# Two decode layers on one Trainium2 core: two more units of a V kept in place, w2 in six places, and the loads of the next K and wq cut in other pieces

## The chip, the cores and the metric

The kernel runs on one core of one Trainium2 chip. The metric is the device time in microseconds (us) of that core. Every program has one launch, and the times are medians of a few runs.

## The reference, cut to what matters

One token (B = 1, one query position, D = 512) goes through two layers of the same weights. Each layer is an attention block and a dense block, each with a layer norm in front and a residual sum behind. All numbers are float32.

```python
def A(x, k_cache, v_cache, wq, wo):          # 32 heads, 4096 keys, 128 wide
    q = (x @ wq).reshape(B, Sq, H, Dh).transpose(0, 2, 1, 3)
    p = softmax(einsum("bhqd,bhkd->bhqk", q, k_cache) * Dh ** -0.5)
    o = einsum("bhqk,bhkd->bhqd", p, v_cache)
    return o.transpose(0, 2, 1, 3).reshape(B, Sq, H * Dh) @ wo

def B(x, w1, b1, w2, b2):                    # 1376 hidden
    return gelu_tanh(x @ w1 + b1) @ w2 + b2

for layer in range(2):
    x = x + A(layernorm(x))
    x = x + B(layernorm(x))
```

The K and V caches have 64 MB each and are read by both layers, so nearly all of the work is reading them.

## The kernel before, in words

**Tiling.** The heads are taken in 8 groups (g = 0 to 7) of 4. The K of a group is one block of 128 partitions by 16384 floats (BLOCK, 8 MB), and so is its V. A block is 8 chunks of NC = 2048 floats (1 MB), a chunk is 4 units of U = 512 floats (256 KB). For each group the kernel makes the queries, multiplies them with the chunks of K (`scores`, L232, on TensorE), takes the softmax (L236 to L254, with the exponential on ScalarE in L244), weighs V with it, sums over the keys and multiplies with the group's wo into the PSUM bank pB (`head_out`). Layer 0 takes the groups upward; layer 1 takes them downward, 7, 6, 5 and so on, so that what layer 0 had last is still in SBUF. Groups in the middle weigh V on ScalarE and VectorE (L269, L274) and sum it there (L279); the first two of layer 1 and the last two of each layer multiply it on TensorE (`values`, L262).

**The arena.** All large data lies in one SBUF tensor, `arena`, addressed by hand: three blocks, of which the third ends early and goes over into the places SPARE (2 chunks), HELD (w1) and PAIR (2 chunks, a wo and a wq). At the end of layer 0 the K of group 7 lies in chunks 0 to 7, its V in chunks 8 to 15, and the V of group 6 (the second last) from chunk 16. Its first five chunks (STAY) stay there until layer 1 needs them. Of the rest, KEPT = 6 units are carried over: five are copied by ScalarE into the PSUM banks pK (L540) and one into pB (L606), since w2, w1 and others take their places in the meantime. In layer 1 they are copied back to the places in V1_HOME: pB's by L506 during the first group's softmax, pK's by L484. What was not kept is loaded again (L482).

**The change of layer.** At the end of layer 0 SP loads, in this order, the last pieces of V, wo, and then w1 in three parts and w2 in five (W2_PARTS), of 11 blocks of one unit. w2 lies in SPARE, in eight places (W2_AT, block c in place c % 8); the third of five parts waits for the reading of `row` (the sum of the heads, L332), which lies in place 7. `mlp` multiplies the 11 blocks (L414), with some idle products in between that keep TensorE busy. `follow` names loads that are issued behind the product of a block: with block 3, 5, 7 and 9 go the last two parts of w2 and into the places that came free the first chunk of the K of group 6 and the wq of group 6. Then layer 1 begins: `set_x` (L166, L167), four query blocks of 8 products each (L199) with wq of group 7, which lies in PAIR's second chunk, and between the second and the third the product of the mean (`minus_mean`, L178), the centred x and its squares (L185, L186). `first_queries` transposes the products (L205) and takes the mean off (L206); `rstd_of` has the product of the variance (L175). Then come the scores of group 7, 64 products in all.

**Order.** All loads are issued by SP into one queue, with `load` holding them in the written order. A load waits until what lay at its target has been read. Instructions marked `pin` stay behind whatever was written before them on their engine; all others are ordered by the framework, ahead of time, by when they are ready and by how late they may be. Each engine then runs its list in order, so what stands behind a waiting instruction waits too. The products of L199 and the four of the mean are not pinned, L175 and the scores are. DMAs take turns on eight semaphores, so a load also waits for the eighth before it.

Of the kernel before, what the change touches and what calls it, by code (L numbers as in the profile page):

```python
# [21 lines left out]
G = 8  # L22
# [6 lines left out]
KEPT = 6  # L29

# [11 lines left out]
K2_HOME = 12 * NC  # L42

V1_HOME = *(2 * BLOCK + NC * c for c in range(5)), 8 * NC, 6 * NC, 7 * NC
W2_AT = tuple(SPARE + U * (c % 8) for c in range(FB)), tuple(U * c for c in range(FB))
# [15 lines left out]
def decode_layers(ctx: ExitStack, tc: tile.TileContext, k, v, w, w1, w2, out):  # L61
# [33 lines left out]

    def of_w(first, n):

        row, i = first
        return w[row][:, AHEAD + NC * i : AHEAD + NC * (i + n)]
# [7 lines left out]
    def free_now(layer, n):  # L107

        if layer == 0:
            at = HELD + 2 * NC  # L110
        elif n == 0:
            at = 6 * NC
            return arena[:, at : at + U], arena[:, 11 * NC : 11 * NC + 4 * 129]
        else:
            at = 9 * NC if n == 1 else 14 * NC
# [65 lines left out]
    def mean_of(xs, s, at, whole=False, xc=None):  # L181
        nm = minus_mean(s, at, whole)
        sq, ss = small("sq", 4), small("ss")
# [3 lines left out]
        return nm, ss, xc  # L187
# [23 lines left out]
    def queries(n, xc, wt, at, t=None, short=False, between=None):  # L211
        t = wt[:, 0, :] if t is None else t
        pin(nc.vector.tensor_scalar(t, wt[:, 0, :], xc[:, 0:1], None, op0=ALU.mult))
        for c in range(1, 4):
            pin(nc.vector.scalar_tensor_tensor(t, wt[:, c, :], xc[:, c : c + 1], t, op0=ALU.mult, op1=ALU.add))  # L215
# [14 lines left out]
    def scores(z, c, kt):  # L230
        for j in range(J):
            pin(nc.tensor.matmul(pS[32 * j : 32 * j + C, :], z[:, j, C - 1 - c : 2 * C - 1 - c],  # L232
                                 kt[:, j, :], start=(c == 0), stop=(c == C - 1)))
# [206 lines left out]
    for layer in range(2):  # L440
# [4 lines left out]
        else:  # L445
            for c in range(4):
                query_block(c, xs, wq_first)
                if c == 1:
                    nm, ss, xc = mean_of(xs, s, pN[:, 0:1])
        if layer == 1:  # L450
            for a in (0, NC // 2):
                load(PAIR + NC + a, part(k, order[1], 1, 2)[:, a : a + NC // 2])
            here["k", order[1], 1] = chunk(arena[:, PAIR + NC : PAIR + 2 * NC])
            negm = small("negm")
            nc.vector.tensor_copy(negm, nm)
            z = first_queries(negm)
# [7 lines left out]
        for n, g in enumerate(order):  # L464
# [13 lines left out]
            elif layer == 1 and n == 1:  # L478
                tiles = [(c, here["k", g, c]) for c in range(2)]
                tiles += list(stream("k", g, ((2, 3), (3, 4), (4, 8)), -2 * NC))  # L480
                n_kept = STAY + U * KEPT
                load(V1_HOME[6] + n_kept % NC, v[g][:, n_kept:BLOCK])  # L482
                for u in range(STAY, n_kept - U, U):
# [30 lines left out]
            elif layer == 1 and n == 1:  # L514
# [3 lines left out]
                for pieces, base in ((((0, 4),), K2_HOME), (((4, 6),), SPARE - 4 * NC)):  # L518
# [169 lines left out]
```

## Time and profile before

| what | us |
|---|---|
| median of 3 runs | 675.73 |
| the runs | 673.7 to 676.0 |
| span of the profiled execution | 671.6 |
| TensorE busy | 299.7 |
| VectorE busy | 407.1 |
| ScalarE busy | 215.4 |

The profiled execution's own time is recorded as its span, 671.6 us from the first to the last instruction; nothing around it is in the trace. The core read 284.92 MB, 424 GB/s over the span. Times below are in us from the start of the span. The change of layer lies between about 342 and 415. Rows give, where they are of DMAs, the moment of issue; the landing is that moment plus the time to landing.

### The profile page before, as it was taken

How to read it: one execution, taken by the hardware profiler on the slowest of the kernel's cores; microseconds unless marked ns; L12 is line 12 of the kernel's file. 1: busy time of each engine (PE TensorE's matmuls, PEld its weight loads, DVE VectorE, ACT ScalarE, POOL GpSimd, SP SyncE). 2: the span in 40 equal slices, each digit the busy share in tenths (PEclk: the TensorE clock that was granted, in tenths of full speed). 3: DMA queues.
4: the chain of work that ended last, by engine and by line, in shares of the span. 5: the costliest groups of instructions: out<-in, count | busy, mean ns of one | idle time of the engine just before them, and what ended most of it. 6: DMA issues, size and time to landing. Idle time of an engine off the chain costs nothing.

```text
span 671.6 us, 6013 instructions
## 1 busy us (share of the span) xinstructions
PE 299.7 (45%) x2236; PEld 79.7 (12%) x2236; DVE 407.1 (61%) x510; ACT 215.4 (32%) x697; POOL 5.2 (1%) x26
## 2 busy tenths in 40 slices
PE   1511703415116053165768986704316025065597
PEld 1000100101001010011114311101001001011124
DVE  3059679498696886971322313288597694973513
ACT  0047074190560823802011200083290650910010
POOL 1000000000000000000000000000000000000000
PEclk9965755757558557578689998655757559557799
DMA  9999999999999999999999999999999999999997
GB/s 377 437 437 438 435 437 437 403 461 437 437 437 397 444 426 434 433 429 426 425 415 399 422 422 438 437 433 433 431 433 437 437 430 402 462 426 414 431 414 286
DMA packets 11556, 285.29 MB, mean 425 GB/s; under 512 B 1284, under 2 KB 1288, under 8 KB 3720
## 3 DMA queue, kind: packets, MB, share of 16 engines
q1 hardware_dynamic: 11528, 284.92, 99.1%
q8 instruction: 17, 0.28, 0.2%
q14 instruction: 11, 0.09, 0.0%
HBM read 284.92 MB, written 0.00 MB: 424 GB/s over the span
## 4 chain that ended last, share of the span: by engine, by line
DMA 64%; PE 17%; DVE 15%; issue 1%; another core or an unknown queue 1%; SPq 1%; ACT 0%; DVEq 0%; ACTq 0%
DMA arena<-in_v 37%; DMA arena<-in_k 24%; PE pS L232 8%; DVE arena L274 7%; PE pO L262 5%; DMA arena<-in_w 4%; DVE arena L279 3%; DVE arena L311 2%; PE pO L283 1%; DVE arena L287 1%; DVE arena L215 1%; SPq L87 1%; PE pB L323 1%; DVE arena L309 0%
## 5 line engine op out<-in xcount | busy, mean ns | idle before, releaser
L269 ACT ACTIVATE arena<-arena,pt 128x128 f32<-128x128 f32 x640 | 188.0, 387 | 50.8 <-DMA arena<-in_v 48.1
L232 PE MATMUL pS<-arena,smalls 128*8 128x512 f32 x1024 | 147.0, 727 | 78.4 <-DMA arena<-in_k 74.3
L279 DVE TENSOR_TENSOR arena<-arena 128x4096 f32<-128x4096 f32 x30 | 132.6, 4420 | 0.3
L274 DVE TENSOR_TENSOR arena<-arena,pt 128x2048 f32<-128x2048 f32 x40 | 89.0, 2287 | 36.8 <-DMA arena<-in_v 35.7
L217 PE MATMUL pS<-arena,smalls 128*128 128x512 f32 x20 | 20.7, 1140 | 202.5 <-DVE arena L215 202.5
L244 ACT ACTIVATE arena<-pS,smalls 128x512 f32<-128x512 f32 x16 | 12.4, 777 | 289.4 <-DVE smalls L243 289.4
L287 DVE STREAM_TRANSPOSE arena<-pO 128x512 f32<-128x512 f32 x16 | 11.5, 717 | 97.4 <-PE pO L262 61.9
L262 PE MATMUL pO<-arena,pt 128*4 128x512 f32 x368 | 48.9, 666 | 11.8 <-DMA arena<-in_v 11.0
L232 PEld LDWEIGHTS pS<-arena,smalls 128*8 128x8 f32 x1024 | 29.8, 102 | 198.6 <-issue 177.3
L236 DVE TENSOR_REDUCE smalls<-pS 128x1 f32<-128x512 f32 x16 | 11.0, 687 | 64.1 <-PE pS L232 64.1
L215 DVE SCALAR_TENSOR_TENSOR arena<-arena,smalls 128x512 f32<-128x512 f32 x45 | 33.8, 752 | 1.6
L311 DVE SCALAR_TENSOR_TENSOR arena<-arena,smalls 128x512 f32<-128x512 f32 x39 | 29.3, 752 | 1.4
L217 PEld LDWEIGHTS pS<-arena,smalls 128*128 128x128 f32 x20 | 5.0, 311 | 206.2 <-DVE arena L215 206.2
L315 PE MATMUL pB<-arena,smalls 128*1 128x512 f32 x26 | 14.7, 648 | 29.0 <-DVE arena L311 29.0
L246 PE MATMUL pO<-ident,arena 128*128 128x128 f32 x64 | 13.4, 344 | 28.1 <-ACT arena L244 27.8
L574 DVE TENSOR_TENSOR arena<-arena 128x2048 f32<-128x2048 f32 x10 | 22.9, 2292 | 0.3
L382 ACT ACTIVATE smalls<-smalls 128x4 f32<-128x4 f32 (+1 forms) x6 | 1.2, 205 | 44.0 <-DVE smalls L375 25.6
L262 PEld LDWEIGHTS pO<-arena,pt 128*4 128x4 f32 x368 | 9.8, 93 | 44.8 <-issue 42.4
L250 DVE STREAM_TRANSPOSE smalls<-smalls 128x32 f32<-128x32 f32 x16 | 3.4, 212 | 17.5 <-ACT arena L244 17.5
L246 PEld LDWEIGHTS pO<-ident,arena 128*128 128x128 f32 x64 | 8.4, 167 | 42.1 <-ACT arena L244 36.7
L244 ACT ACT_TABLE_LOAD x1 | 1.3, 1283 | 36.9 <-DVE smalls L243 36.9
L438 PE MATMUL pS<-arena,ident 128*8 128x256 f32 (+1 forms) x34 | 11.9, 454 | 0.5 <-DVE pt L367 0.5
(115 smaller groups left out, 183.6 us busy)
## 6 DMA issues: line engine op xcount, KB each, us to landing
arena<-in_w SPq DMA_DIRECT2D x13, 2048.0 KB, 12.5
arena<-in_k SPq DMA_DIRECT2D x6, 4096.0 KB, 21.3
arena<-in_v SPq DMA_DIRECT2D x2, 4096.0 KB, 25.1
arena<-in_w SPq DMA_DIRECT2D x6, 1024.0 KB, 30.9
arena<-in_v SPq DMA_DIRECT2D x2, 2048.0 KB, 37.0
arena<-in_k SPq DMA_DIRECT2D x2, 2048.0 KB, 13.4
arena<-in_w SPq DMA_DIRECT2D x7, 512.0 KB, 9.3
arena<-in_v SPq DMA_DIRECT2D x3, 1024.0 KB, 46.3
```

The costliest lines, as they stand in the source:

```text
L215: pin(nc.vector.scalar_tensor_tensor(t, wt[:, c, :], xc[:, c : c + 1], t, op0=ALU.mult, op1=ALU.add))
L217: pin(nc.tensor.matmul(at, one.to_broadcast([P, P]), t, start=True, stop=True))
L232: pin(nc.tensor.matmul(pS[32 * j : 32 * j + C, :], z[:, j, C - 1 - c : 2 * C - 1 - c], kt[:, j, :], start=(c == 0), stop=(c == C - 1)))
L246: nc.tensor.transpose(pT[:, b].rearrange("p j r -> p (j r)"), p[:, P * b : P * (b + 1)], ident)
L262: nc.tensor.matmul(pO[32 * j : 32 * j + 4, :], pt[:, j, c, :], by_head(vt)[:, j], start=(i == 0), stop=(i == of - 1))
L269: nc.scalar.activation(own, own, AF.Copy, scale=pt[:, j, c, b : b + 1])
L274: nc.vector.tensor_tensor(own, own, weight, op=ALU.mult)
L279: pin(nc.vector.tensor_tensor(a, a, b, op=ALU.add))
L287: nc.vector.transpose(ot[:, :512], pO)
L311: pin(nc.vector.scalar_tensor_tensor(t, wt[:, d, :], on[:, d : d + 1], t, op0=ALU.mult, op1=ALU.add))
L315: pin(nc.tensor.matmul(pB[0:1, :], one, t, start=n == 0, stop=n == G - 2))
L574: pin(nc.vector.tensor_tensor(total, total, other, op=ALU.add))
```

## The change

Two more units of group 6's V, the last two of its seventh chunk, stay where they landed (INPLACE = 2): places 6 and 7 of SPARE are no longer used for w2, which goes round in six places. `row` moves to place 4, so the part (4,6) of w2 now waits for its reading; the part (6,8) moves from that point into `follow`, and the others move back by one step. Group 6's wq goes into places 5, 0, 1 and 4, its K is cut into units 0 and 1 (places 2 and 3), 2 to 5 (where the wq of group 7 lay), 6 to 9, 10 to 13 and 14 to 31 (the first 26 units of the arena), and `scores` takes lists of units. The V that is loaded again shrinks to units 28 to 31. The K of the third group of layer 1 (g = 5) comes in 6 chunks at once and 2 later, instead of 4, 2 and 2. pK's fifth unit and pB's go back to places 4 and 5 instead of a place in the old K. In the first queries of layer 1, the product of the mean comes behind all four query blocks, the mean is read from PSUM without a copy, and the centred x and its squares are written behind `first_queries`.

```diff
@@ -27,6 +27,7 @@
 EPS = 1e-5
 U = 512
 KEPT = 6
+INPLACE = 2
 
 NC = 4 * U
 BLOCK = 8 * NC
@@ -39,10 +40,10 @@
 SMALLS = 324
 AHEAD = 64
 X_AT, B1_AT, B2_AT = 0, 8, 8 + FB
-K2_HOME = 12 * NC
-
-V1_HOME = *(2 * BLOCK + NC * c for c in range(5)), 8 * NC, 6 * NC, 7 * NC
-W2_AT = tuple(SPARE + U * (c % 8) for c in range(FB)), tuple(U * c for c in range(FB))
+K2_HOME = 10 * NC
+
+V1_HOME = *(2 * BLOCK + NC * c for c in range(5)), 8 * NC, SPARE + NC, 7 * NC
+W2_AT = tuple(SPARE + U * (c % 6) for c in range(FB)), tuple(U * c for c in range(FB))
 PITCH = 1024
 W2_PARTS = ((0, 4), (4, 6), (6, 8), (8, 10), (10, FB)), ((0, 4), (4, 8), (8, 10), (10, FB))
 HIDDEN = ((0, 4), (4, 8), (8, FB))
@@ -93,6 +94,13 @@
     def chunk(t, i=0):
         return t[:, NC * i : NC * (i + 1)].rearrange("p (j n) -> p j n", j=4)
 
+    def unit(t, j):
+
+        return t[j] if isinstance(t, list) else t[:, j, :]
+
+    def units(*places):
+        return [arena[:, at : at + U] for at in places]
+
     def of_w(first, n):
 
         row, i = first
@@ -109,8 +117,8 @@
         if layer == 0:
             at = HELD + 2 * NC
         elif n == 0:
-            at = 6 * NC
-            return arena[:, at : at + U], arena[:, 11 * NC : 11 * NC + 4 * 129]
+            at, ot_at = 6 * NC + 2 * U, 9 * NC + 3 * U - 4
+            return arena[:, at : at + U], arena[:, ot_at : ot_at + 4 * 129]
         else:
             at = 9 * NC if n == 1 else 14 * NC
         return arena[:, at : at + U], arena[:, at + U : at + U + 4 * 129]
@@ -180,11 +188,14 @@
 
     def mean_of(xs, s, at, whole=False, xc=None):
         nm = minus_mean(s, at, whole)
+        return nm, *spread(xs, nm, xc)
+
+    def spread(xs, nm, xc=None):
         sq, ss = small("sq", 4), small("ss")
         xc = small("xc", 4) if xc is None else xc
         nc.vector.tensor_scalar(xc, xs[:, :, 0], nm, None, op0=ALU.add)
         nc.vector.scalar_tensor_tensor(sq, xc, 1.0, xc, op0=ALU.mult, op1=ALU.mult, accum_out=ss)
-        return nm, ss, xc
+        return ss, xc
 
     def rstd_of(ss, at, whole=False):
         nv = minus_mean(ss, at, whole)
@@ -209,10 +220,10 @@
 
 
     def queries(n, xc, wt, at, t=None, short=False, between=None):
-        t = wt[:, 0, :] if t is None else t
-        pin(nc.vector.tensor_scalar(t, wt[:, 0, :], xc[:, 0:1], None, op0=ALU.mult))
+        t = unit(wt, 0) if t is None else t
+        pin(nc.vector.tensor_scalar(t, unit(wt, 0), xc[:, 0:1], None, op0=ALU.mult))
         for c in range(1, 4):
-            pin(nc.vector.scalar_tensor_tensor(t, wt[:, c, :], xc[:, c : c + 1], t, op0=ALU.mult, op1=ALU.add))
+            pin(nc.vector.scalar_tensor_tensor(t, unit(wt, c), xc[:, c : c + 1], t, op0=ALU.mult, op1=ALU.add))
         if short:
             pin(nc.tensor.matmul(at, one.to_broadcast([P, P]), t, start=True, stop=True))
             if between is not None:
@@ -230,7 +241,7 @@
     def scores(z, c, kt):
         for j in range(J):
             pin(nc.tensor.matmul(pS[32 * j : 32 * j + C, :], z[:, j, C - 1 - c : 2 * C - 1 - c],
-                                 kt[:, j, :], start=(c == 0), stop=(c == C - 1)))
+                                 unit(kt, j), start=(c == 0), stop=(c == C - 1)))
 
     def softmax(sc, nsc, p, hold):
         top = nc.vector.tensor_reduce(mx[:, 0:1], pS, axis=AX.X, op=ALU.max)
@@ -445,15 +456,10 @@
         else:
             for c in range(4):
                 query_block(c, xs, wq_first)
-                if c == 1:
-                    nm, ss, xc = mean_of(xs, s, pN[:, 0:1])
-        if layer == 1:
-            for a in (0, NC // 2):
-                load(PAIR + NC + a, part(k, order[1], 1, 2)[:, a : a + NC // 2])
-            here["k", order[1], 1] = chunk(arena[:, PAIR + NC : PAIR + 2 * NC])
-            negm = small("negm")
-            nc.vector.tensor_copy(negm, nm)
-            z = first_queries(negm)
+            nm = minus_mean(s, pN[:, 0:1])
+            load(PAIR + NC, k[order[1]][:, 2 * U : 6 * U])
+            z = first_queries(nm)
+            ss, xc = spread(xs, nm)
         xc_l = small("xc_l", 4)
         r = rstd_of(ss, pN[:, 1:2], True)
         nc.vector.tensor_copy(xc_l, xc)
@@ -476,11 +482,15 @@
             if layer == 1 and n == 0:
                 tiles = [(c, here["k", g, c]) for c in range(C)]
             elif layer == 1 and n == 1:
-                tiles = [(c, here["k", g, c]) for c in range(2)]
-                tiles += list(stream("k", g, ((2, 3), (3, 4), (4, 8)), -2 * NC))
-                n_kept = STAY + U * KEPT
-                load(V1_HOME[6] + n_kept % NC, v[g][:, n_kept:BLOCK])
-                for u in range(STAY, n_kept - U, U):
+                for a, b in ((6, 10), (10, 14), (14, 32)):
+                    load(U * (a - 6), k[g][:, U * a : U * b])
+                late_at = PAIR + NC
+                tiles = [(0, units(SPARE + 2 * U, SPARE + 3 * U, late_at, late_at + U)),
+                         (1, units(late_at + 2 * U, late_at + 3 * U, 0, U))]
+                tiles += [(c, chunk(arena[:, U * (4 * c - 6) : U * (4 * c - 2)])) for c in range(2, C)]
+                n_kept = STAY + U * (KEPT + INPLACE)
+                load(V1_HOME[n_kept // NC], v[g][:, n_kept:BLOCK])
+                for u in range(STAY, STAY + U * (KEPT - 1), U):
                     nc.scalar.copy(v_next(u), pK[(u - STAY) // U])
                 for c in range(STAY // NC, C):
                     here["v", g, c] = chunk(arena[:, V1_HOME[c] : V1_HOME[c] + NC])
@@ -515,9 +525,8 @@
                 for c in range(C):
                     values(c, pt, here["v", g, c], c)
 
-                for pieces, base in ((((0, 4),), K2_HOME), (((4, 6),), SPARE - 4 * NC)):
-                    for _ in stream("k", order[2], pieces, base):
-                        pass
+                for _ in stream("k", order[2], ((0, 6),), K2_HOME):
+                    pass
             elif final:
                 last_v = chunk(arena[:, v_home + BLOCK - NC : v_home + BLOCK])
                 for _ in range(FILL - 1 if layer == 1 else 0):
@@ -586,10 +595,9 @@
             if final:
                 if layer == 0:
                     row_to_quadrants(row)
-                    for a, b in W2_PARTS[0][1:3]:
-                        load(W2_AT[0][a], w2[:, U * a : U * b])
-                        if a == 4:
-                            load(HELD + W1_AT[2], w1[:, W1_AT[2] :])
+                    a, b = W2_PARTS[0][1]
+                    load(W2_AT[0][a], w2[:, U * a : U * b])
+                    load(HELD + W1_AT[2], w1[:, W1_AT[2] :])
                 idle(last_v, pO, 256)
             head_out(on, wo_t, n)
             if final:
@@ -599,7 +607,7 @@
                             True)
             if n == G - 2:
 
-                row = arena[:, HELD - U : HELD] if layer == 0 else p
+                row = arena[:, SPARE + NC : SPARE + NC + U] if layer == 0 else p
                 nc.vector.tensor_copy(row, pB)
                 if layer == 0:
                     u = STAY + U * KEPT - U
@@ -617,13 +625,13 @@
             xb = of_32(ends, 4)
         follow = {}
         if layer == 0:
-            first_k, next_wq = part(k, G - 2, 0, 1), of_w(wq_at(G - 2), 1)
+            next_k, next_wq = k[G - 2], of_w(wq_at(G - 2), 1)
+            part_2, part_3, part_4 = ((W2_AT[0][a], w2[:, U * a : U * b]) for a, b in W2_PARTS[0][2:])
             follow = {
-                3: (*((W2_AT[0][a], w2[:, U * a : U * b]) for a, b in W2_PARTS[0][3:]),
-                    (SPARE + NC - U, first_k[:, NC - U :])),
-                5: ((SPARE + NC, next_wq[:, : 2 * U]),),
-                7: ((SPARE + NC + 2 * U, next_wq[:, 2 * U :]),),
-                9: ((SPARE, first_k[:, : 2 * U]),),
+                3: (part_2, part_3),
+                5: (part_4, (SPARE + 5 * U, next_wq[:, :U])),
+                7: ((SPARE, next_wq[:, U : 3 * U]),),
+                9: ((SPARE + 2 * U, next_k[:, : 2 * U]),),
             }
         mlp(x1, s1, w1_t, w2_t[layer], xb, *((None, last_v) if layer == 0 else (ends, None)), follow)
         if layer == 0:
@@ -631,11 +639,9 @@
             mt = work.tile([P, P], F32, name="pt")
             nc.vector.transpose(mt, pM)
             xs, s = set_x(of_32(mt, 4), 1.0, xb, True)
-            g = G - 2
             wq_first = wq_next
-            wq_next = chunk(arena[:, SPARE + NC : SPARE + 2 * NC])
-            load(SPARE + 2 * U, first_k[:, 2 * U : NC - U])
-            here["k", g, 0] = chunk(arena[:, SPARE : SPARE + NC])
+            load(SPARE + 4 * U, next_wq[:, 3 * U :])
+            wq_next = units(SPARE + 5 * U, SPARE, SPARE + U, SPARE + 4 * U)
     xb_rows, y = ends[:, P : 2 * P], ends[:, 2 * P :]
     nc.vector.tensor_tensor(y, pM, xb_rows, op=ALU.add)
     nc.sync.dma_start(out, y[0:P:32, :])
```

## Rows read from the trace of the kernel before

**Rows 1.** Page, 40 slices: busy tenths of the DMA engines.

```profile
DMA  9999999999999999999999999999999999999997
```

**Rows 2.** Windows: stretch, length, busy time by engine (count), clock, DMA share, GB/s.

```profile
10.00:340.00 330.00, 118.93 (x694) 28.50 (x694) 221.77 (x232) 125.32 (x408) 0.57 (x1) 0.67 1.00 431
...
366.00:372.00 6.00, 4.74 (x94) 2.46 (x98) 2.14 (x15) 1.69 (x3) 0.73 (x2) 1.00 0.98 356
...
0.00:1.70 1.70, 0.00 (x0) 0.00 (x0) 0.75 (x4) 0.00 (x0) 0.80 (x9) 1.00 0.00 0
...
354.00:362.00 8.00, 7.46 (x122) 3.83 (x120) 1.60 (x9) 0.20 (x1) 0.94 (x3) 1.00 1.01 414
```

**Rows 3.** Chain of waits in order of time: start, duration, what.

```profile
0.72 4.95 DMA arena<-in_w
...
369.91 0.15 PE pO L178 x7
...
371.15 7.05 PE pS L232 x64
...
656.04 11.41 DMA arena<-in_w
```

**Rows 4.** Timeline of SP: issue, length (merged: to the last one's end), target.

```profile
354.11 0.33 SPq L87 DMA_DIRECT2D arena<-in_w  x1
...
360.60 1.27 SPq L87 DMA_DIRECT2D arena<-in_w  x1
...
364.64 2.57 SPq L87 DMA_DIRECT2D arena<-in_w  x2
368.25 0.33 SPq L87 DMA_DIRECT2D arena<-in_k  x1
...
370.48 0.33 SPq L87 DMA_DIRECT2D arena<-in_k  x1
372.25 0.33 SPq L87 DMA_DIRECT2D arena<-in_k  x1
...
376.55 0.33 SPq L87 DMA_DIRECT2D arena<-in_k  x1
...
390.21 0.33 SPq L87 DMA_DIRECT2D arena<-in_k  x1
...
414.61 0.33 SPq L87 DMA_DIRECT2D arena<-in_v  x1
```

**Rows 5.** DMA issues at 360.60, 364.64 and 366.88: KB, us to landing.

```profile
arena<-in_w SPq DMA_DIRECT2D x1, 256.0 KB, 7.5
...
arena<-in_w SPq DMA_DIRECT2D x1, 512.0 KB, 5.4
...
arena<-in_w SPq DMA_DIRECT2D x1, 512.0 KB, 4.4
```

**Rows 6.** Timelines of PE and DVE at layer 1's start: start, duration, engine, line.

```profile
370.59 0.38 PE L175 MATMUL pO<-smalls 128*128 128x1 f32 x2 [0.16 <-DVE smalls L186]
...
370.09 0.23 DVE L185 TENSOR_SCALAR smalls<-smalls,pO 128x4 f32<-128x4 f32 x1 [0.73 <-PE pO L178]
...
370.36 0.16 DVE L186 SCALAR_TENSOR_TENSOR smalls<-smalls 128x4 f32<-128x4 f32 x1
...
370.52 0.31 DVE L205 STREAM_TRANSPOSE pt<-pS 128x128 f32<-128x128 f32 x1
370.87 0.23 DVE L206 SCALAR_TENSOR_TENSOR smalls<-pt,smalls 128x4 f32<-128x4 f32 x1
```

**Rows 7.** Timeline in the first group's softmax of layer 1, ACT and PE.

```profile
377.38 0.59 ACT L506 COPY arena<-pB 128x512 f32<-128x512 f32 x1 [9.23 <-PE pS L232]
...
380.08 0.78 ACT L244 ACTIVATE arena<-pS,smalls 128x512 f32<-128x512 f32 x1 [2.12 <-DVE smalls L243]
...
380.69 1.05 PE L226 MATMUL pO<-smalls,arena 128*128 128x1 f32 x8
```

**Rows 8.** Window of the scores at the lower clock: PE busy (count), loads, clock.

```profile
425.10:430.30 5.20, 5.20 (x28) 1.02 (x32) 0.50 0.96 416
```

## The prediction

> **What bounds the kernel now.** I read the page's slices first, then windows, then the chain of waits, then the queue of DMA issues. The slices show the DMA engines at nine tenths or more in 39 of 40 [rows 1]; the windows show a share of 1.00 and 431 GB/s over the long stretch of the first layer [rows 2]. All loads go through one queue that SP issues in a written order, so the kernel ends when the last byte has landed: the chain runs into a DMA from 656.04 to 667.45, and only some 4 us of arithmetic and the output follow [rows 3]. Time can be gained in two ways, by moving fewer bytes or by letting the queue run dry less; compute matters only where it frees a buffer so late that the queue is empty. The reader is to see one weak stretch: from 366 to 372 the engines are 0.98 busy but move 356 GB/s, since the loads there are short rows, pieces of 256 and 512 KB [rows 2]. That is the change of layer, which the diff rewrites.
>
> The profiled execution is known by its span, 671.6; the median of the shown runs, 675.73, lies 4.1 above it. I carry these 4.1 over and add differences to the median.
>
> **Bytes.** With KEPT + INPLACE = 8 units instead of 6, the load of the rest of group 6's V shrinks from 1536 to 1024 KB. No other size in total changes: w2, wq and K are cut differently. 524,288 bytes at the 431 GB/s of the steady stretch [rows 2] are 1.22 us. The pieces change too. Two 512 KB loads issued at 364.64 and 366.88 (the second issue ends 2.57 after 364.64 and takes 0.33) landed 1.3 us apart, at 364.64 + 5.4 and 366.88 + 4.4 [rows 4, 5], 0.06 to 0.08 more than at 431 GB/s. Before, the K and wq pieces of this stretch are two of 256 KB and five of 512 KB; after, two of 256 and two of 512, then loads of 1 MB and more. Three 512 KB pieces fewer are 0.2 us. Together -1.4 us (bounds -1.2, rate alone, and -1.6), on every engine, since each load is spread over all.
>
> **The queue at the change of layer.** The saving stands only if the queue does not run dry. What a load needs I bound from the start of the program: the load issued at 0.72 had no packet moving before 1.70 [rows 2], and its 1056 KB, 2.5 us at 431 GB/s, took 4.95 to land [rows 3], 2.4 more. So a load must be issued between 1.0 and 2.4 us before its predecessor lands, or a hole opens; I take 1.5, nearer to the lower end, because the 2.4 holds the cold first packets of the program. The Trainium skill ("DMA: Bandwidth & Descriptors", Specifications) gives about 0.6 us to the first byte for this path; the trace is slower, 1.0, and by 0.6 no hole would open at all and the sum would be the bare -1.4.
>
> Now the landings after, one by one. W2 in six places means that (6,8) can no longer be issued ahead; it goes behind the product of w2 block 3, with (8,10), where (10,11) was issued before, at 360.60, and (10,11) goes behind block 5, at 364.64. And w2's (4,6), with the last part of w1 behind it in SP's order, now waits until `row` has been read (it lies in place 4), at 354.11, where before (6,8) waited for the same reading [rows 4]. All three cost nothing: the 1 MB loads issued earlier keep the share at 1.01 from 354 to 362 [rows 2], and the bytes up to w2's block 10 come in the same order and number, so this block still lands at 360.60 + 7.5 = 368.1 [rows 4, 5]. Without that cover the late (4,6) would cost up to its own 1.3.
> - wq's first unit (256 KB) lands at 368.75, its middle two (512 KB, issued behind block 7 at 366.88 as its like before) at 370.05.
> - K's first two units wait for block 9, 368.25 [rows 4]: 1.8 us ahead, enough. They land at 371.35, wq's last unit at 372.0. Before, two 512 KB and a 256 KB load more stood in the queue here; that cushion is gone.
> - K's units 2 to 5 (1 MB over the old wq) wait for the last query product. Before, the second half was let go at 370.48 [rows 4]; with the mean's four products (0.15 [rows 3]) behind instead of between, about 370.4. 1.6 us ahead: just enough. Lands at 374.5.
>
> **The mean behind the queries** takes the copy of the mean out (counted at nothing, since other vector work stands around it), but it also moves that vector work. Before, L185 and L186 ran while PE still did the last queries, the variance's product L175 stood done from 370.59 + 0.38, and the scores went off at 371.15 behind L206 [rows 3, 6]. After, the transpose comes first, then L206, L185 and L186 in one order or another, all behind the mean. L175 is held in program order ahead of the scores, so PE's scores wait for it. The transpose (0.31) would end at about 370.76, a little earlier than before; then 0.23 for L206, 0.27 from start to start for L185 and about 0.25 for L186 with its accumulator [rows 6]: if L206 is last, scores at 371.6; if L186 is last, 371.55 + 0.38 of L175, 371.95. So x, the delay of the first head's scores, is 0.5 to 0.8 us; I take 0.65 (bound below: -0.1, if only the shorter queries showed). Queued behind L175 on PE are all scores, and SP's next loads wait for those:
> - K units 6 to 9, before released at 372.25 [rows 4], at 372.9: 1.6 ahead of 374.5. Lands at 377.0, units 10 to 13 at 379.4.
> - Units 14 to 31 now reach into the seventh chunk of the old K, so they wait for one chunk of scores more: 376.55 [rows 4] + 0.88 (an eighth of 7.05 [rows 3]) + 0.65 = 378.1, 1.3 ahead of 379.4. A hole of 0.2. 4.5 MB land at 390.6, the shorter rest of V at 393.1.
> - K of the third group, now 6 MB in one, waits as before for the first head's values: 390.21 [rows 4] + 0.65 = 390.9, 2.2 ahead. It lands at 407.7, the weights behind it at 412.5, K's last quarter at 417.4.
> - The next V, 414.61 [rows 4] + 0.65 = 415.3: 2.1 ahead. From here on the loads stand in the queue long before their turn and the shift is carried to the end.
>
> Holes: 0.2 by these numbers; since the engines do not run in step I set 0.3. With 1.0 needed there is none, with 2.4 there are 0.6, 0.25 and 0.25, so 1.1. A smaller x, or L206 last, lies inside this.
>
> **Sum.** -1.4 + 0.3 = -1.1: span 670.5, time 674.6. Bounds -1.6 and -0.1: 674.1 to 675.6.
>
> **Rivals.**
> - *Late starts eat the saving.* A load that comes to a nearly empty queue pays the whole 2.4 us. For it: four loads have less than 2 us of lead, where before the shortest were about 3 (366.88 against a landing at 370.0 [rows 4, 5]). Against it: from 366 to 372 the share stayed at 0.98 with pieces as small [rows 2]. Holes of 1.1 and a little: -0.3, 675.4. The Trainium skill ("DMA: Bandwidth & Descriptors", Anatomy of one DMA) puts the fixed part of a DMA at about 2.0 us, for another issuing path; by that the holes would be 0.6 and the time 674.9. The one empty start of this trace is dearer, so it leans the rule's way.
> - *Slower: the kept unit's copy holds up the softmax.* ACT's copy of the unit parked in pB (L506) went at 377.38. Its target is now wq's first unit, in which the next queries are summed, so it must wait for PE's L226, 380.69 + 1.05 [rows 7]. If ACT has it in front of the exponential (380.08 [rows 7]), that starts at 382.35, 2.3 late, and with it the first head's values and the 6 MB load: 393.2 against a landing at 393.1, a hole of 1.6. Net -1.1 + 1.6 = +0.5: 676.2. It turns the sign from a delay of the exponential of about 1.7. For it: the copy stands first in the program and was first before. Against: the order given to ACT follows readiness, and the exponential is ready 1.7 us sooner.
> - *Slower: the clock.* The scores ran at clock 1.00; at 0.50 a chunk took 5.20/28 instead of 7.05/64 us per product [rows 3, 8]. If the longer pause before the scores lost the clock, units 14 to 31 would be let go 4.2 us later still, a hole of about 4: +3, 678.8, more if the values are caught too. Against: the clock stood at 1.00 from 366 to 372 through pauses like this [rows 2].
>
> **Chances.** Forecast 0.62, late starts 0.20, copy 0.09, clock 0.04, and 0.05 that the gain is larger than I count. The three shown runs of one kernel are 2.3 apart, more than the whole effect, so the range is 672.8 to 677.0: bounds of the sum and the copy's case with about a microsecond for the runs on either side. A change of 0.5% (3.4 us, about what a measurement of this kernel can tell from none) needs more than the bytes give; only the clock's case and half of the unexplained larger gain with stray runs lie beyond: faster 0.06, same 0.89, slower 0.05.
>
> **What would show it.** Right: in the profile after, 0.52 MB less read; the V load 1024 KB; scores of the first head starting at 371.5 to 372; DMA share from 366 to 380 not under 0.95; the last w2 load landing 0.8 to 1.4 earlier against the span's start. The copy L506 behind the exponential. Wrong: a stretch of GB/s clearly under 350 between 370 and 380 or a gap before the 4.5 or 6 MB load (late starts); the exponential of the first head past 382 (copy); a clock under 1.00 between 370 and 380. A span shorter by over 2 us would mean that loads ran faster for a reason I have not priced.

## The result and the profile after

The kernel after takes 675.33 us (median of 22 runs, 674.33 to 678.08), the kernel before, run beside it on the same chip, 673.87 (22 runs). The ratio is 1.0019, with an interval of [1.0012, 1.0027]: 1.3 us slower, with 0.8 to 1.8 inside the interval, where 1.1 us faster was forecast. The profiled execution took 675.78, its span is 674.0 (before 671.6). All ratios below are against runs of the kernel before on the same chip; a ratio of 1.0015 is 1.0 us.

In the kernel after, L87 has become L88 (load), L175 L183, L178 L186, L185 L196, L186 L197, L205 L216, L206 L217, L226 L237, L232 L243, L244 L255, L506 L516.

The bytes went as forecast. The page after says:

```profile
span 674.0 us, 6007 instructions
...
DMA  9999999999999999999999999999999999999996
...
HBM read 284.39 MB, written 0.00 MB: 422 GB/s over the span
```

0.53 MB less is read, and the slices look as full as before [rows 1]. At 17 us a slice they are too coarse to show what follows. The windows do (length, busy time of PE, weight loads, DVE, ACT, POOL, then clock, DMA share and GB/s; a packet counts whole in the window in which it starts, so a share can pass 1). After:

```profile
360.00:386.00 26.00, 21.91 (x304) 9.37 (x306) 8.70 (x33) 4.57 (x10) 1.19 (x5) 1.00 0.98 361
386.00:650.00 264.00, 123.53 (x737) 27.22 (x730) 163.62 (x191) 84.40 (x276) 0.00 (x0) 0.68 1.00 431
...
364.00:370.00 6.00, 4.19 (x94) 2.19 (x95) 1.51 (x7) 1.90 (x4) 0.48 (x3) 1.00 0.89 312
370.00:376.00 6.00, 4.89 (x78) 2.24 (x82) 3.56 (x14) 0.00 (x0) 0.55 (x1) 1.00 0.97 319
...
365.30:366.10 0.80, 0.68 (x36) 0.46 (x25) 0.00 (x0) 0.00 (x0) 0.00 (x0) 1.00 0.80 307
...
366.00:380.00 14.00, 11.35 (x152) 4.36 (x153) 5.49 (x19) 2.28 (x4) 0.84 (x3) 1.00 0.93 321
```

Before, in the same stretches:

```profile
360.00:386.00 26.00, 22.80 (x304) 8.89 (x298) 8.41 (x33) 5.73 (x12) 1.02 (x4) 1.00 1.03 408
386.00:650.00 264.00, 123.25 (x738) 27.21 (x734) 163.53 (x191) 83.05 (x273) 0.00 (x0) 0.69 1.00 431
...
364.00:370.00 6.00, 4.45 (x125) 2.65 (x128) 1.15 (x5) 1.69 (x3) 0.29 (x2) 1.00 0.99 366
370.00:376.00 6.00, 5.66 (x66) 1.76 (x61) 3.90 (x14) 0.00 (x0) 0.55 (x1) 1.00 1.03 392
...
365.30:366.10 0.80, 0.41 (x24) 0.19 (x12) 0.26 (x1) 0.00 (x0) 0.10 (x1) 1.00 1.05 402
```

The reader is to see that nothing has changed from 386 on (431 GB/s in both) and that the change of layer moves 361 GB/s instead of 408. 26 us x 47 GB/s are 1.22 MB, 2.8 us at 431 GB/s. Less the 1.2 us that the missing 512 KB are worth, 1.6 are left; 1.3 were measured. The two profiled spans differ by more, by 2.4. Counted in bytes still to come, the execution after is 1.4 to 1.8 us behind at every point from 120 MB to 1 MB before the end, so nothing is lost on the way; the rest arises in the last microseconds of these two executions.

Two things arrive late. The chain of waits after (start, length):

```profile
365.22 3.58 DMA arena<-in_w
368.80 0.04 issue
368.84 0.44 PE pO L425 x8
...
370.03 1.04 PE pS L210 x30
371.06 0.06 PE pO L186 x7
...
371.15 0.33 DVE pt L216
...
371.57 0.23 DVE smalls L217
371.80 0.15 DVE smalls L196
...
371.98 0.18 DVE smalls L197 x2
...
372.20 0.38 PE pO L183 x2
372.58 6.98 PE pS L243 x64
```

W2's last part (block 10) is now on the chain: it lands at 368.80, not at 368.1, its products wait for it, and the query products start at 370.03. The mean's vector work, L196 and L197, and its product L183 follow the transpose one after another, and the first scores (a timeline gives 372.51) go off 2.48 after the queries. Before it was 371.15 [rows 3], 1.84 after them. So the scores are 1.36 late, 0.7 by block 10 and 0.64 by the mean.

SP's issues after (start, length, merged to the last one's end) answer to [rows 4]:

```profile
361.22 0.80 SPq L88 DMA_DIRECT2D arena<-in_w  x2
...
365.22 0.33 SPq L88 DMA_DIRECT2D arena<-in_w  x1
...
368.27 0.33 SPq L88 DMA_DIRECT2D arena<-in_k  x1
369.30 0.33 SPq L88 DMA_DIRECT2D arena<-in_w  x1
371.14 0.33 SPq L88 DMA_DIRECT2D arena<-in_k  x1
...
378.74 0.33 SPq L88 DMA_DIRECT2D arena<-in_k  x1
...
391.57 0.33 SPq L88 DMA_DIRECT2D arena<-in_k  x1
```

The DMA issues (KB each, us from issue to landing) at 361.66 (the second of the first line), 365.22, 368.27, 369.30, 371.14, 378.74 and 391.57, beside [rows 5]:

```profile
arena<-in_w SPq DMA_DIRECT2D x1, 512.0 KB, 5.8
...
arena<-in_w SPq DMA_DIRECT2D x1, 256.0 KB, 3.6
...
arena<-in_k SPq DMA_DIRECT2D x1, 512.0 KB, 5.1
...
arena<-in_w SPq DMA_DIRECT2D x1, 256.0 KB, 4.8
...
arena<-in_k SPq DMA_DIRECT2D x1, 1024.0 KB, 7.7
...
arena<-in_k SPq DMA_DIRECT2D x1, 4608.0 KB, 16.0
...
arena<-in_k SPq DMA_DIRECT2D x1, 6144.0 KB, 20.2
```

The small load at 365.22 has only the end of one load ahead of it (361.66 + 5.8 = 367.46), and still takes 3.6 us; what the landings mean for the forecast follows below.

And ACT's timeline answers to [rows 7]:

```profile
381.44 0.78 ACT L255 ACTIVATE arena<-pS,smalls 128x512 f32<-128x512 f32 x1 [4.29 <-DVE smalls L254]
...
383.14 0.59 ACT L516 COPY arena<-pB 128x512 f32<-128x512 f32 x1 [0.84 <-PE pO L237]
```

The copy stands behind the exponential, and the clock is 1.00 throughout: neither the copy's rival nor the clock's came.

### The profile page after: what moved, and what is told of

It is laid out like the page before. It is cut to its first block, busy times and chain, and to the rows that moved or that the text cites. A ratio compares the mean times of both kernels' runs of the same rounds, so it can differ in the third digit from the quotient of the medians.

```text
span 674.0 us, 6007 instructions
## 1 busy us (share of the span) xinstructions
PE 303.6 (45%) x2236; PEld 80.6 (12%) x2236; DVE 407.2 (60%) x509; ACT 215.4 (32%) x697; POOL 5.2 (1%) x26
## 4 chain that ended last, share of the span: by engine, by line
DMA 57%; PE 21%; DVE 17%; another core or an unknown queue 2%; issue 1%; SPq 0%; ACT 0%; DVEq 0%; ACTq 0%
DMA arena<-in_v 31%; DMA arena<-in_k 23%; PE pS L243 9%; DVE arena L285 7%; PE pO L273 6%; DVE arena L290 3%; DMA arena<-in_w 3%; DVE arena L322 2%; DVE arena L226 1%; DVE arena L298 1%; PE pO L294 1%; PE pS L449 1%; PE pO L257 1%; PE pB L334 1%
## 5 line engine op out<-in xcount | busy, mean ns | idle before, releaser
L243 PE MATMUL pS<-arena,smalls 128*8 128x512 f32 x1024 | 147.5, 729 | 78.4 <-DMA arena<-in_k 74.4
L255 ACT ACTIVATE arena<-pS,smalls 128x512 f32<-128x512 f32 x16 | 12.4, 778 | 294.1 <-DVE smalls L254 294.1
L273 PE MATMUL pO<-arena,pt 128*4 128x512 f32 x368 | 51.8, 700 | 9.9 <-DMA arena<-in_v 8.8
L243 PEld LDWEIGHTS pS<-arena,smalls 128*8 128x8 f32 x1024 | 29.6, 102 | 199.1 <-issue 178.5
L226 DVE SCALAR_TENSOR_TENSOR arena<-arena,smalls 128x512 f32<-128x512 f32 x45 | 33.8, 752 | 1.6
## 6 DMA issues: line engine op xcount, KB each, us to landing
arena<-in_k SPq DMA_DIRECT2D x1, 6144.0 KB, 20.2
```

Of the source, the lines that this page charges most:

```text
L226: pin(nc.vector.scalar_tensor_tensor(t, unit(wt, c), xc[:, c : c + 1], t, op0=ALU.mult, op1=ALU.add))
L273: nc.tensor.matmul(pO[32 * j : 32 * j + 4, :], pt[:, j, c, :], by_head(vt)[:, j], start=(i == 0), stop=(i == of - 1))
```

## The experiments

Theory going in: the bytes are worth what was counted, and the loss comes from loads that come too late for their queue at the change of layer. The rivals are the mean alone, the larger pieces alone, block 10's late part alone, and, later, that a unit kept in place takes a place from the loads in advance. At the end one table holds all the numbers against one another.

**The mean back between the queries** (kernel after, L458 on):

```
+    if c == 1:
+        nm, ss, xc = mean_of(xs, s, pN[:, 0:1])
-nm = minus_mean(s, pN[:, 0:1])
 load(PAIR + NC, k[order[1]][:, 2 * U : 6 * U])
-z = first_queries(nm)
-ss, xc = spread(xs, nm)
+negm = small("negm")
+nc.vector.tensor_copy(negm, nm)
+z = first_queries(negm)
```

> The changed kernel, but with the mean's products, its copy and the centred x between the second and the third query block, as before. Theory A (the queue of loads runs dry at the change of layer, since the engines run up to 2.4 us apart and a load needs about 3 us of lead, not 1.5): the scores of the first head start about 0.65 us earlier, the loads behind them are let go earlier by as much, and a part of the holes closes: 674.3 to 675.0, ratio to before 1.0006 to 1.0016. Rival B (the mean's place alone made the kernel slower than forecast, 2.8 us dearer than the bytes saved): about 672.5, ratio 0.998. Rival C (the holes come from w2 and the pieces alone and the scores' start does not matter): 675.3, ratio 1.002.

Measured: 1.0017 [1.0008, 1.0026]. The slowdown stays, so the mean is not its cause alone. In the profiled execution block 10's part landed only at 369.55, the scores began at 372.60, and 352 GB/s were moved.

**The mean behind the queries, alone** (kernel before, the same edit in the other direction).

> The kernel before, with nothing changed but the mean's products behind all four query blocks, read from PSUM, and the centred x behind the first queries. Theory A: scores of the first head 0.6 us later; the queue's leads of about 3 us shrink by that and open small holes: +0.2 to +0.6, ratio 1.0003 to 1.0009. Rival B (the mean alone): +2 or more, ratio above 1.003. Rival C: no change, ratio 1.000.

Measured: 1.0005 [0.9996, 1.0014], not told apart from no change. The scores began at 371.80, the 0.65 later that the forecast took.

**The bytes alone** (kernel before; the two units of V are left out of the load and read as they lie):

```
-load(V1_HOME[6] + n_kept % NC, v[g][:, n_kept:BLOCK])
+load(V1_HOME[7], v[g][:, n_kept + 2 * U:BLOCK])
```

> The kernel before, leaving out the loading of two units of the second last V (they are read unloaded, so the output is off): 512 KB less and nothing else changed. If bytes saved in this stretch reach the end, as the prediction had it: -1.2 to -1.5 us, ratio 0.9978 to 0.9982. Rival D (the time of this stretch is set by compute and the saved transfer is hidden anyway): ratio 1.000.

Measured: 0.9994 [0.9985, 1.0002]; the same kernel once more on another chip,

> The third experiment once more (the kernel before without the loading of two units of V, values off), since its interval did not settle it. Theory G (that transfer is behind the stretch that is short of room, so it counts in full): -1.0 to -1.5 us, ratio 0.9978 to 0.9985. Rival D (hidden anyway): 1.000.

gave 0.9988 [0.9978, 0.9997]. The bytes are worth 0.4 and 0.8 us by these ratios; the second interval holds 1.2, the first does not.

**Smaller pieces** (the first experiment, and besides):

```
-load(PAIR + NC, k[order[1]][:, 2 * U : 6 * U])
+for u in (2, 4):
+    load(PAIR + NC + U * (u - 2), k[order[1]][:, U * u : U * (u + 2)])
...
-for a, b in ((6, 10), (10, 14), (14, 32)):
+for a, b in ((6, 10), (10, 14), (14, 22), (22, 32)):
```

> The first experiment's kernel with K's units 2 to 5 loaded in two halves (the first needs only the first two query blocks) and units 14 to 31 as 14 to 21 and 22 to 31 (the first needs four chunks of scores, not seven). Theory A: two releases come 0.5 and 2.6 us earlier; another part of the holes closes, 0.4 to 0.9 us better than the first experiment: ratio to before 0.9995 to 1.0008. Rival C' (the holes lie ahead of these loads, at w2's last parts and wq): like the first experiment.

Measured: 1.0006 [0.9991, 1.0021]; 382 GB/s, scores at 371.08. Block 10's part, issued and placed as in the first experiment, landed at 368.01, 1.5 earlier: its landing scatters between executions, so the two profiles don't give the price of the pieces, and the intervals overlap.

**Block 10's part issued earlier** (kernel after, into the place of a kept V unit):

```
-W2_AT = tuple(SPARE + U * (c % 6) ...
+W2_AT = tuple(SPARE + U * (6 if c == 10 else c % 6) ...
-3: (part_2, part_3),
-5: (part_4, (SPARE + 5 * U, next_wq[:, :U])),
+3: (part_2, part_3, part_4),
+5: ((SPARE + 5 * U, next_wq[:, :U]),),
```

> The changed kernel, but w2's block 10 goes into place 6, over a kept unit of V (whose values are then off), so that its load is issued behind block 3 as before and not behind block 5. Nothing else is moved. Theory A (the queue runs dry first at 365, where the last part of w2 is let go with 2.2 us of lead, lands 0.7 to 1.5 us later than before, and holds up block 10, the end of layer 0 and all releases behind it): scores of the first head 0.7 us earlier than in the changed kernel, 674.3 to 674.9, ratio to before 1.0003 to 1.0012. Rival F (the holes are set by the mean and by K's pieces; w2's last part is waited for without harm): 675.1 to 675.4, ratio 1.0015 to 1.002.

Measured: 1.0015 [1.0005, 1.0026]. The part landed at 367.86, and the scores began at 371.58, 0.93 earlier than after, yet the time hardly moved: from 370 to 376 it still moved only 332 GB/s. That being early helps little while the loads behind still come late is argued, not shown.

**Everything as early as before** (the fourth experiment's kernel with block 10's part as in the last experiment and wq in two halves):

```
-5: (part_4, (SPARE + 5 * U, next_wq[:, :U])),
-7: ((SPARE, next_wq[:, U : 3 * U]),),
+5: ((SPARE + 4 * U, next_wq[:, : 2 * U]),),
+7: ((SPARE, next_wq[:, 2 * U :]),),
```

> The fourth experiment's kernel (mean between the queries, finer pieces of K) with w2's block 10 in place 6 over a kept unit (values off), so that w2 has seven places, wq's units go two behind block 5 and two behind block 7, and nothing is left to load behind block 10. Theory A: the lead is that of the kernel before nearly everywhere, and the 512 KB saved come through: 672.6 to 673.5, ratio 0.9980 to 0.9993. Rival F: like the fourth experiment, ratio 1.000.

Measured: 1.0008 [0.9998, 1.0018]. It issues its loads at the points of the kernel before, but for two units of K (512 KB) that went there behind w2's blocks 3 and 10 and have no place here; its scores begin at 371.24, 0.1 later than before. By every step of the forecast it had to gain 1.2. Its windows show where that is lost:

```profile
364.00:370.00 6.00, 4.48 (x121) 2.61 (x124) 1.15 (x5) 1.70 (x4) 0.29 (x2) 1.00 0.94 340
370.00:376.00 6.00, 5.66 (x77) 1.77 (x62) 3.90 (x14) 0.59 (x1) 0.55 (x1) 1.00 0.88 277
376.00:382.00 6.00, 5.83 (x38) 1.91 (x30) 2.02 (x9) 1.00 (x3) 0.00 (x0) 1.00 1.05 438
```

The queue was emptied sooner, because there was less in it, and what comes next waits for the same buffers at the same time: the first half of K's units 2 to 5 goes at 370.08, 2.8 us ahead of the landing before it, where its like in the kernel before goes at 369.99, 3.5 ahead.

**A full version with seven places** (one more unit kept in place, not two, so 256 KB saved; the mean between the queries; smaller pieces): `INPLACE = 1`, seven places in `W2_AT`, `W2_PARTS` (0, 4), (4, 6), (6, 7), (7, 9), (9, FB), and the K units 3 to 6, 7 to 10 and so on.

> A full version with one more unit of V in place instead of two (256 KB saved), w2 in seven places with its last part issued behind block 3, the mean between the queries and K in finer pieces. Theory A: 0.65 us of bytes saved, of which up to 0.4 are given back in holes: 673.4 to 673.9, ratio 0.9991 to 1.0000, faster than both kernels if barely. Rival F: 674.3, ratio 1.0005.

Measured: 1.0007 [0.9998, 1.0017]. Half the bytes, for half the places, give no gain either. No version that keeps the whole computation beat the kernel before.

**Late scores alone** (kernel before):

```
+for _ in range(4 if layer == 1 else 0):
+    idle(last_v, pS)
 late = None
```

> The kernel before with four idle products of 512 columns ahead of layer 1's scores, which start about 1.6 us later; no load is changed. The queue's leads at this place fall from about 3 to 1.5 us. Theory A (a load needs about 3 us of lead): holes of 0.8 to 1.6 us, 674.8 to 675.6, ratio 1.0011 to 1.0024. The prediction's figure (1.5 us of lead are enough): at most 0.3, ratio 1.0000 to 1.0005.

Measured: 1.0036 [1.0024, 1.0047], 2.4 us. The delay was larger than planned. PE's timeline has the four as eight records, two of each, seven of them in the first line, and the first K load behind the scores went at 375.20, not at 372.25 [rows 4]:

```profile
370.66 3.17 PE L438 MATMUL pS<-arena,ident 128*8 128x512 f32 x7
...
373.24 0.61 PE L232 MATMUL pS<-arena,smalls 128*8 128x512 f32 x3
373.67 0.59 PE L438 MATMUL pS<-arena,ident 128*8 128x512 f32 x1
```

2.95 us of delay cost 2.4 (1.6 to 3.2). In the kernel before, these loads (372.25, 373.11, 376.55) go 5.3 to 6.8 us ahead of their predecessor's landing; the delay left 2.1 to 3.8, and that was too little. So of such a lead some 0.5 us are spare, at most 1.3.

**More room in the kernel before** (1 MB of K in advance, over a kept part of V): `(2 * BLOCK, part(k, G - 2, 2, 3))` behind w2 block 3.

> The kernel before, with one chunk of the next K (1 MB) loaded early, behind w2's last part, over a chunk of the kept V (whose values are then off) instead of waiting for the scores. Same bytes, 1 MB more room for loads in advance. Theory G (at the change of layer the queue holds all that there is room for, and a unit kept in place is a unit of loads in advance lost): the kernel before has small holes left, -0.3 to -1.0 us, ratio 0.9985 to 0.9996. Rival (the stretch is not short of room): 1.000.

Measured: 0.9998 [0.9989, 1.0006]. Theory G missed: the profiled execution moved 421 GB/s at the change of layer, but the time shows no gain, or one of at most 0.7 us. More room is worth little to the kernel before.

**The same room in the kernel after** (units 6 to 9 of K in advance, over a kept part of V): `(2 * BLOCK, next_k[:, 6 * U : 10 * U])` behind block 5.

> The changed kernel with the same 1 MB of room: K's units 6 to 9 are loaded behind w2's last part over a chunk of the kept V (values off) instead of behind the first scores. Theory G: most of the holes behind 368 close (those at 365 stay, w2's last part is still late) and the saved bytes begin to show: 1.2 to 2.0 us better than the changed kernel, ratio to before 0.9990 to 1.0004. Rival H (the delay is the compute chain's, the engines' order, or the larger pieces, and more loads in advance would not help): ratio 1.0015 to 1.002 as the changed kernel.

Measured: 1.0015 [1.0003, 1.0026]; its profiled execution was the fastest of its twelve. Windows:

```profile
370.00:376.00 6.00, 4.91 (x58) 1.56 (x54) 3.97 (x13) 0.34 (x1) 0.55 (x1) 1.00 1.04 414
376.00:382.00 6.00, 6.00 (x39) 1.92 (x30) 1.89 (x7) 1.12 (x3) 0.00 (x0) 1.00 0.96 358
```

The hole from 370 to 376 is gone and another has opened later (358 GB/s from 376 to 382, where the kernel before has 444), before the 4.5 MB load, which waits for its buffer to 377.75, 2.75 ahead of its predecessor's landing.

**The same room with everything as early as before** (the sixth experiment with that 1 MB behind block 3):

> The sixth experiment's kernel (seven places for w2, mean between, finer pieces) with the same 1 MB of room. Theory G: nearly no holes, so that the 512 KB saved come through whole: -0.9 to -1.6 us against before, ratio 0.9976 to 0.9987. Rival H: as the sixth, 1.0008.

Measured: 0.9984 [0.9975, 0.9992], at least as much as the bytes alone give (0.9994 and 0.9988). Its windows, against those of the sixth experiment:

```profile
364.00:376.00 12.00, 10.18 (x180) 4.36 (x184) 4.99 (x20) 2.48 (x5) 0.96 (x4) 1.00 1.02 391
...
370.00:376.00 6.00, 5.66 (x80) 1.95 (x74) 3.70 (x14) 0.59 (x1) 0.55 (x1) 1.00 1.06 407
376.00:382.00 6.00, 6.00 (x38) 1.95 (x30) 2.18 (x8) 0.87 (x2) 0.00 (x0) 1.00 1.00 412
```

277 GB/s became 407, and the two intervals don't touch. The only difference is 1 MB that could be issued some 9 us sooner (363.17 is its issue), into a place that no working kernel has free, since a part of the kept V lies there. No hole follows at 376 to 382 as in the last experiment: units 14 to 31 come in two loads here, and the first goes at 375.13, 5.8 ahead of the landing before it.

**All together.** Worked out: 26 us times the rate missing to 408 GB/s between 360 and 386, at 431 GB/s, less 0.0024 us for each KB saved. Measured: the ratio times 674.

| kernel | GB/s, 360 to 386 | worked out, us | measured, us |
|---|---|---|---|
| after | 361 | +1.6 | +1.3 (0.8 to 1.8) |
| mean between | 352 | +2.2 | +1.1 (0.5 to 1.8) |
| mean behind alone | 397 | +0.7 | +0.3 (-0.3 to 0.9) |
| bytes alone, two chips | 399, 408 | -0.7, -1.2 | -0.4 (-1.0 to 0.1), -0.8 (-1.5 to -0.2) |
| smaller pieces | 382 | +0.3 | +0.4 (-0.6 to 1.4) |
| block 10 early | 376 | +0.7 | +1.0 (0.3 to 1.8) |
| all as early as before | 368 | +1.2 | +0.5 (-0.1 to 1.2) |
| seven places, 256 KB | 380 | +1.1 | +0.5 (-0.1 to 1.1) |
| late scores | 363 | +2.7 | +2.4 (1.6 to 3.2) |
| room, before | 421 | -0.8 | -0.1 (-0.7 to 0.4) |
| room, after | 394 | -0.4 | +1.0 (0.2 to 1.8) |
| room, all early | 402 | -0.9 | -1.1 (-1.7 to -0.5) |

The rate comes from one execution of each kernel, the time from eight or more, and single executions of one kernel lie 0.6 to 5 us apart. In nine of the twelve rows the worked-out time lies within the measured interval; the mean between, room in the kernel before and room in the kernel after miss it, by 0.1 to 0.6. The profiled execution was the slowest of its eleven for the mean between and the fastest of its twelve for room in the kernel after. The rows on which the cause rests, bytes alone and the two with everything early, agree.

## Why the prediction was wrong, point by point

- **"I carry these 4.1 over".** Wrong by 2.3: every execution on record lies 1.7 to 2.0 above its span, so the profiled one of the kernel before stood near 673.4, and its 22 runs have 673.87, not 675.73. So it is luck that 675.33 lies inside the stated range, and that it lies beside the 675.4 of the late starts; against the kernel before, the sign was wrong.
- **Bytes, -1.4.** Right in direction and somewhat too large: 0.4 and 0.8 measured where nothing else was changed. The 0.2 for fewer short pieces is too small for any of these runs to show; the packets bear it out, a packet of 4 KB taking 160 ns in both traces (median), which makes 1.28 us for 512 KB on 16 engines against 1.22 at 431 GB/s.
- **"So a load must be issued between 1.0 and 2.4 us before its predecessor lands, or a hole opens; I take 1.5".** This is the step that failed, and with it "Holes: 0.2 by these numbers". 2.8 us of rate were lost against the kernel before, not 0.3. The predecessor's landing tells when the last of 16 engines is through; the others have run dry before. By the semaphore updates in the trace, one from each engine, the 512 KB issued at 361.66 are through on the first engine at 365.78 and on the last at 367.46 (5.8 after the issue), and from 365.30 to 366.10 the share is 0.80. The part issued at 365.22 had 2.2 us of lead by its predecessor's landing but 0.6 to the first engine, and its own first packet moved 1.0 after its issue: it was late. Units 2 to 5 had 3.0 of lead when they were issued (their predecessor landed at 369.30 + 4.8), twice what the step asked for, but 0.9 to the first engine (372.04), and 370 to 376 moved 319 GB/s. In the kernel before, the load at 372.25 has 5.3 and 2.6. How much is enough the runs do not give: in the sixth experiment 2.8 by the landing and 1.5 to the first engine (370.08) still went with a hole.
  The landings that the forecast reckoned one by one slipped: block 10's part 0.7, K's first units 2.0 (368.27 + 5.1 = 373.4), units 2 to 5 4.3 (371.14 + 7.7 = 378.8 instead of 374.5), units 14 to 31 4.1 (378.74 + 16.0 = 394.7 instead of 390.6), and the 6 MB load 4.1 (391.57 + 20.2 = 411.8 instead of 407.7). About half of the 4.1 is not the change's: the kernel before lands the last of this K at 376.55 + 16.1 = 392.7, later than the 390.6 that the forecast gave the changed one, for the list ran the stretch at 431 GB/s, and the kernel before moves 408 in it. So the leads were reckoned from landings that were too early, and the one hole of the list did not come where it was put: units 14 to 31 went 5 us ahead of the landing before them, not 1.3.
- **Its lower and upper end.** The 1.0 from issue to first packet came again (365.22 to 366.18, of which 0.33 is the issuing instruction). The 2.4 from the start of the program was taken for the cold end. It was the nearer one: the 256 KB issued at 365.22 took 3.58 us to land, 3.0 more than at 431 GB/s, in part because the last engine had the load ahead until 367.46. The Trainium skill ("DMA: Bandwidth & Descriptors", Anatomy of one DMA) puts the fixed part at about 2.0 us for another issuing path. No run here shows that figure: the one load that came to an empty queue, the program's first, took 2.4 more than its bytes.
- **"All three cost nothing ... so this block still lands at 360.60 + 7.5 = 368.1".** Wrong by 0.7 in the profile after, by 1.4 in the first experiment, by nothing in the fourth (368.01). Issued 4.6 us later than before and behind less, the part had no cover left, and its landing scatters.
- **x, the delay of the first head's scores by the mean, 0.65.** Right: 0.64 after, 0.65 in the experiment on it alone. Its price alone is at most 0.9 and not told apart from none.
- **The rival "late starts eat the saving"** was the right one, at 0.20 and with the wrong size: 675.4 assumed holes of 1.1 between loads. It turns the sign at holes of 1.4, and it was never worked out that far, because the lead was measured to the wrong event.
- **The signs to watch for.** "DMA share from 366 to 380 not under 0.95" came out at 0.93, but 370 to 376 alone, with 319 GB/s, would have passed at 0.97; "GB/s clearly under 350 between 370 and 380" shows it plainly. The scores began at 372.51, after the 372 of the right case, and the last w2 load landed 2.4 later than before, not 0.8 to 1.4 earlier. A packet that lasts longer than the steady ones counts as busy all the while, so the share hides more than half of such a hole. Counted from the two traces' packets, an engine is idle for 1.5 us between 360 and 386 (before 0.2) and loses 2.8 (before 1.0) to packets that last longer than the median of their size; together 3.0 more than before.

What lies behind the failed step is space. The two units kept in place occupy places into which w2 block 10, more of wq and the next K went in advance, and every load that loses its place waits for compute. That is shown by the pair of the sixth and the eleventh experiment: the saving of 512 KB without the room gives no gain (1.0008), with 1 MB of room it gives all (0.9984). That the same room brings the kernel before nothing that its interval shows (0.9998) fits a kernel that has nearly enough.

Room alone does not do it in the kernel after (1.0015). Its 4.5 MB load, units 14 to 31 in one, waits for the seventh chunk of scores, and there the next hole opened; in the eleventh experiment, with these units in two loads, none did. That the larger piece is the reason is read from two profiles, and no run changes it alone. What stays open is how the loss divides among the late block 10, the mean and the larger pieces: taken singly, the runs put 0.3, 0.1 and 0.7 us on them (fifth experiment against after, first against after, fourth against first), each with an uncertainty of about 1 us.

## What to carry to other kernels

In a kernel that ends with its last byte, a buffer kept in place saves bytes and takes room from loads in advance: before counting the bytes, list which loads lose their place and how late they then go. Measure the lead of a load to the moment at which the first engine of the queue runs dry, which a window of a microsecond shows, not to its predecessor's landing; here 2 to 3 us by the landing was too little, while the kernel before has 3.1 and more for its loads from 366 on. Once the lead is used up, a delay of the release costs most of its length (2.4 us of 2.95 here), though the page's slices stay at nine tenths.

## What the runs showed of the hardware

- The 16 engines of one queue do not keep step: the load issued at 361.66 was through on the first at 365.78 and on the last at 367.46, and with it still 1.4 us from landing the share was 0.80. Half a microsecond before block 10's part lands, a window of the kernel after shows 0.58:

```profile
367.80:368.30 0.50, 0.41 (x16) 0.11 (x5) 0.00 (x0) 0.49 (x2) 0.00 (x0) 1.00 0.58 217
```

- A DMA share of 0.97 went with 319 GB/s, where 1.00 goes with 431 in the steady stretch; the share alone does not tell whether a queue keeps up.
- A product of 512 columns that was put in as idle work took 0.86 us, two records of 0.43 (eight from 370.66 on, the last begun at 373.67). The scores' 64 records are 32 products, so one of them takes 0.22 (7.05 / 32 [rows 3]): an idle product is no small unit of delay.
